# Quarter products for w_v, and the next batch's mixing placed inside the w_k product

## Chip, cores and metric

One core of a Trainium2 chip runs the whole kernel. The metric is the device time of one execution in microseconds (us). A matmul runs on TensorE (PE; its weight loads are PEld), element-wise work on VectorE (DVE), ScalarE (ACT) and GpSimd (POOL); transfers are issued from SyncE's queue (SPq) and ScalarE's (ACTq).

## What is computed

Three layers follow one another on 8 batches of 576 tokens. All matrices are float32.

```
x   = rmsnorm(q @ (k^T v)) * g                      # per head, 8 heads of 64 -> 512 features
xk  = mu_k*x + (1-mu_k)*x_prev                      # x_prev: x one token earlier
xr  = mu_r*x + (1-mu_r)*x_prev
kk  = max(xk @ w_k, 0)                              # w_k: 512 x 1024
x2  = sigmoid(xr @ w_r) * (kk*kk @ w_v)             # w_r: 512 x 512, w_v: 1024 x 512
out = mixture of 4 causal attention experts of x2   # top 2, weights from a gate
```

## The kernel before

A float32 matmul is replaced by three matmuls of the float32r type: each operand x is split into a high part (ScalarE rounds it) and a low part (VectorE subtracts: `split`, L58), and high*high, high*low and low*high are summed in PSUM (`mm3`, L62). The work runs in three stages.

`phase_a` (L174) goes over the batches. `front(b)` (L242) forms k^T v (40 products from five pairs of loads kt, vt), applies it to q in four bursts (`heads`, L268), sums squares with TensorE (`means`, L285), computes the reciprocal root on VectorE in 14 small operations (`rsqrt`, L295) and multiplies it into the tile xT (`scaled`, L316, which spreads the root over partitions by TensorE, L321). `mix_r(b)` makes xr in the tiles xrh, xrl (four rounds of L356 on ScalarE, L357 on VectorE, then a split); `mix_k(b)` makes xk and its operands. `r_group` (L411) is a gate: 12 matmuls, a sigmoid and, per pair of halves, a store to sgd; a batch has eight. `k_pair` (L425) is the w_k product, a Strassen form with seven quarter products instead of eight: weights as seven blocks A11 to S3 and operands b11, b21, t1, t2, b22, t4, t3, of which the t's are differences of quarters of xk, made on GpSimd (L382). A quarter product for one m is 6 matmuls of 288 columns; four m's times seven make 168 in a batch. VectorE adds the quarter results (L457 to L472), GpSimd clips them at zero (L445) and squares them (L446), and they are stored to kkd.

In the loop over batches (L530) batch b's mixing and gates come first; then the w_k product runs, with `front(b+1)` and, from its 20th step on, `mix_r(b+1)` interleaved step by step. `mix_k(b+1)` comes in the next turn. The tiles xT, xk, xrh, xrl and the operands have one buffer each. The weights arrive as 64-bit words and are rebuilt as float32 pairs by `Conv` (L111): one `tick` works on a piece of 128 x 512 with five VectorE operations (L129 to L138), an absolute value on ScalarE, and either three matmuls ("PE") or two GpSimd operations ("POOL", L161 and L162). w_v's eight pieces are converted in the last turn, after the weights' staging pool has been closed (L560, ticks at L539, L555 and L613).

`phase_v` (L573) multiplies kk*kk with w_v directly: for each batch, two halves of the tokens times four m's, each a group of 24 matmuls (8 K tiles times three) of 288 columns; four operand splits of 128 x 1152 (L593, L595) prepare a batch, and VectorE multiplies each group with its gate (L605). x2d is stored by halves. `phase2` (L627) is the attention stage.

Instructions are written in the order of the generators, and `schedule_with_timeline_sim=True` (L989) lets a planner reorder them on each engine by its own estimate of when each is ready; the program order is the priority. On the chip every engine then runs its list in order.

Of the kernel before, what the change touches and what calls it, by code (L numbers as in the profile page):

```python
# [1 line left out]

# [22 lines left out]
def tile_kernel(ctx: ExitStack, tc: tile.TileContext, qT, k, v, g2, mu_k, mu_r, w_r, w_k, w_v, w_qk, w_vg, w_o, out):  # L25
# [21 lines left out]
    kkd = [dram.tile([P, KF, S], F32, name=f"kkd{i}") for i in range(B)]  # L47
    sgd = [dram.tile([P, KD, S], F32, name=f"sgd{i}") for i in range(B)]
# [62 lines left out]
    class Conv:  # L111


        def __init__(self, pool, wts, bufs):
            self.pool, self.wts, self.bufs = pool, wts, bufs
            self.raws, self.cvs, self.ops, self.at = {}, {}, [], 0

        def load(self, i):
            if i < len(self.wts):
                _, _, w, r0, c0, _ = self.wts[i]  # L120
                raw = self.raws[i] = self.pool.tile([P, CW, 2], I32, name="raw", bufs=self.bufs)
                nc.scalar.dma_start(raw.rearrange("p n t -> p (n t)"), w[r0:r0 + P, c0:c0 + CW].bitcast(I32))

        def words(self, i):
# [9 lines left out]
            nc.scalar.activation(wh, t, AF.Copy)  # L134
# [10 lines left out]
        def tick(self, acc_tile=None, idn=None):  # L145
            i = self.at
            self.at += 1
            if 0 < i <= len(self.wts):
# [11 lines left out]
                else:  # L160
                    nc.gpsimd.tensor_sub(x, x, h.bitcast(F32))  # L161
                    nc.gpsimd.tensor_add(l, x, l.bitcast(F32))  # L162
                self.load(i - 1 + self.bufs)
            if i < len(self.wts):
                t = self.cvs[i] = self.pool.tile([P, CW], F32, name="cvt", bufs=self.bufs)
# [8 lines left out]
    def phase_a():  # L174
        with ExitStack() as st1:
# [20 lines left out]
            a21h = stg.tile([P, 2, 512], F32R, name="a21h")  # L196
            a21l = stg.tile([P, 2, 512], F32R, name="a21l")
# [5 lines left out]
            for blk, r0, c0 in ((A11, 0, 0), (A12, 2, 0), (None, 0, 512), (A22, 2, 512)):  # L203
                for i in range(2):
                    h, l = (a21h, a21l) if blk is None else (wkh[:, blk], wkl[:, blk])
# [3 lines left out]
            def sums(i):  # L209
# [3 lines left out]
                a21 = [(a21h[:, i, :], 1), (a21l[:, i, :], 1)]  # L213
# [140 lines left out]
            def mix(b, p, mu, nu, x):  # L354
                xT = xTs[b]
                nc.scalar.activation(x, xT[:, p, 0:S], AF.Copy, scale=nu[:, p:p + 1])  # L356
                nc.vector.scalar_tensor_tensor(x, xT[:, p, 1:S + 1], mu[:, p:p + 1], x, op0=ALU.mult, op1=ALU.add)  # L357

            def mix_r(b):
                for p in range(KD):  # L360
                    x = sb.tile([P, S], F32, name="xm", bufs=2)
                    mix(b, p, mur, nur, x)
                    split(xrh[:, p, :], xrl[:, p, :], x)
# [3 lines left out]

            def mix_k(b):
# [149 lines left out]
            for i in range(8):  # L518
                r_group(0, *divmod(i, 2))
                run(mk)  # L520
                if i < 6:
                    tick()
# [470 lines left out]
```

## Time and profile before

| | us |
|---|---|
| median of 3 runs (lowest, highest) | 1171.03 (1170.14, 1173.21) |
| the profiled execution, its own time | 1171.94 |
| its span | 1170.1 |
| PE busy | 1017.1 (87%) |
| DVE busy | 617.7 (53%) |
| ACT busy | 486.9 (42%) |
| POOL busy | 436.0 (37%) |

The busy shares are means over stages with different limits, so they say little; the stages have to be read one by one. Matmuls overlap in the trace: a 288-column matmul is shown with 0.29 us, while the next one starts some 0.13 us later at full clock. The page's idle columns tell what ended each wait.

### The profile page before, as it was taken

The page shows a single profiled execution, that of the slowest core. Times are in us where ns is not written, and L with a number is a line of the kernel's source. Part 1 is how long each engine was busy: PE and PEld are TensorE (multiplying, and loading weights), DVE is VectorE, ACT ScalarE, POOL GpSimd, SP SyncE. Part 2 cuts the span into 40 slices and gives each one's busy share as a digit, 9 for nine tenths or more (in the row PEclk, how much of TensorE's full clock was granted, in tenths as well). Part 3 has the DMA queues.
Part 4 walks back from the last instruction along what each step waited for, and adds up shares of the span by engine and source line. Part 5 has one row for each costly group of instructions (what it writes and reads, how often), then busy time and mean ns, then how long its engine had stood idle before and what let it go on. Part 6 is the DMA issues. An engine that isn't in the chain of part 4 may idle for free.

```text
span 1170.1 us, 20536 instructions
## 1 busy us (share of the span) xinstructions
PE 1017.1 (87%) x7968; PEld 909.9 (78%) x7968; DVE 617.7 (53%) x1508; ACT 486.9 (42%) x1123; POOL 436.0 (37%) x456
## 2 busy tenths in 40 slices
PE   5459796978879796959699999989999999999998
PEld 3248685858777685858599999988888988889887
DVE  5682645455463627288845333315656565565553
ACT  4454443534353534444313112104554463554544
POOL 0021645463636455468910000014453262352521
PEclk8679898988979798989789999999999999999999
DMA  9304242433324151225856655312020120210102
GB/s 317 120 1 144 100 143 102 140 104 113 111 83 161 63 169 53 84 77 181 329 166 233 200 185 163 97 64 60 23 82 24 60 80 4 81 52 32 64 1 81
DMA packets 59312, 127.17 MB, mean 109 GB/s; under 512 B 5712, under 2 KB 23632, under 8 KB 56144
## 3 DMA queue, kind: packets, MB, share of 16 engines
q1 hardware_dynamic: 47888, 105.94, 26.5%
q10 hardware_dynamic: 11328, 19.93, 5.4%
q8 instruction: 63, 1.03, 0.4%
q14 instruction: 33, 0.27, 0.1%
HBM read 78.66 MB, written 47.19 MB: 108 GB/s over the span
## 4 chain that ended last, share of the span: by engine, by line
PE 59%; DVE 16%; POOL 11%; DMA 8%; ACT 5%; issue 3%; ACTq 0%; SPq 0%; POOLq 0%; DVEq 0%
PE acc L64 12%; PE acc L66 11%; PE acc L65 11%; PE acc L434 11%; POOL tk L382 4%; DMA x2in<-x2d 3%; PE pt L812 3%; PE acc L839 2%; POOL so L445 2%; DVE xk L357 2%; DVE xT L324 2%; POOL x2l L649 2%; PE s L763 2%; PE po L275 2%; DMA vt<-in_v 2%
## 5 line engine op out<-in xcount | busy, mean ns | idle before, releaser
L445 POOL TENSOR_SCALAR so<-so 128x576 f32<-128x576 f32 x64 | 108.7, 1702 | 140.4 <-DVE so L463 126.7
L65 PE MATMUL acc<-kkl,wvh 128*128 128x288 f32 x512 | 153.9, 301 | 5.5 <-DVE kkl L595 5.5
L66 PE MATMUL acc<-kkh,wvl 128*128 128x288 f32 x512 | 153.5, 301 | 3.8 <-POOL wvl L162 3.8
L64 PE MATMUL acc<-kkh,wvh 128*128 128x288 f32 x512 | 153.0, 299 | 3.8 <-ACT kkh L593 3.8
L792 POOL TENSOR_SCALAR pr<-pr,rc,wg 128x512 f32<-128x512 f32 (+3 forms) x128 | 76.3, 608 | 98.5 <-DVE wg L722 61.7
L775 ACT ACTIVATE pr<-pr,nm 128x256 f32<-128x256 f32 (+4 forms) x144 | 83.2, 579 | 66.3 <-DVE nm L729 63.1
L65 PEld LDWEIGHTS acc<-kkl,wvh 128*128 128x128 f32 x512 | 99.0, 193 | 6.1 <-DVE kkl L595 6.1
L66 PEld LDWEIGHTS acc<-kkh,wvl 128*128 128x128 f32 x512 | 98.7, 193 | 4.3 <-POOL wvl L162 4.3
L64 PEld LDWEIGHTS acc<-kkh,wvh 128*128 128x128 f32 x512 | 98.8, 193 | 4.2 <-ACT kkh L593 4.0
L321 PE MATMUL po<-rb,selb 32*128 32x144 f32 x128 | 22.2, 435 | 77.2 <-DVE rb L314 44.0
L593 ACT ACTIVATE kkh<-kin 128x1152 fp32r<-128x1152 f32 x32 | 37.1, 1166 | 123.8 <-PE acc L66 112.2
L65 PE MATMUL acc<-xrl,wrh 128*128 128x288 f32 x256 | 78.3, 318 | 8.9 <-DVE xrl L60 8.8
L64 PE MATMUL acc<-xrh,wrh 128*128 128x288 f32 x256 | 69.8, 347 | 14.0 <-ACT sg L419 11.7
L321 PEld LDWEIGHTS po<-rb,selb 32*128 32x128 f32 x128 | 16.7, 303 | 83.4 <-issue 83.4
L64 PE MATMUL acc<-x2h,wqh 128*128 128x256 f32 (+1 forms) x256 | 79.8, 312 | 1.4 <-DVE vs L692 1.0
L65 PE MATMUL acc<-x2l,wqh 128*128 128x256 f32 (+1 forms) x256 | 76.9, 300 | 4.3 <-POOL x2l L649 4.3
L605 DVE TENSOR_TENSOR sgv<-acc,sgv 128x288 f32<-128x288 f32 x64 | 28.9, 455 | 94.4 <-PE acc L66 94.4
L66 PE MATMUL acc<-xrh,wrl 128*128 128x288 f32 x256 | 77.3, 314 | 0.0
L66 PE MATMUL acc<-x2h,wql 128*128 128x256 f32 (+1 forms) x256 | 76.6, 299 | 0.0
L446 POOL TENSOR_TENSOR so<-so 128x576 f32<-128x576 f32 x64 | 75.2, 1184 | 2.5
L729 DVE CUSTOM_DVE_ANT_0 pr<-s,mask 128x256 f32<-128x256 f32 (+4 forms) x144 | 66.9, 482 | 16.4 <-PE pt L812 12.1
L382 POOL TENSOR_TENSOR tk<-xk 128x576 f32<-128x576 f32 x16 | 26.6, 1661 | 107.2 <-DVE xk L357 104.4
(235 smaller groups left out, 3000.5 us busy)
## 6 DMA issues: line engine op xcount, KB each, us to landing
kkd<-so SPq DMA_DIRECT2D x64, 288.0 KB, 2.1
kin<-kkd SPq DMA_DIRECT2D x16, 1152.0 KB, 6.2
qt<-in_qT SPq DMA_DIRECT2D x32, 288.0 KB, 2.9
sgd<-sg SPq DMA_DIRECT2D x32, 288.0 KB, 2.2
sgv<-sgd SPq DMA_DIRECT2D x8, 1152.0 KB, 5.3
x2d<-sgv SPq DMA_DIRECT2D x16, 576.0 KB, 3.6
out<-ob SPq DMA_DIRECT2D x28, 288.0 KB, 2.1
kt<-in_k SPq DMA_DIRECT2D x24, 256.0 KB, 4.3
```

The costliest lines, as they stand in the source:

```text
L64: nc.tensor.matmul(ps, wh(i), xh(i), start=(i == 0), stop=False)
L65: nc.tensor.matmul(ps, wh(i), xl(i), start=False, stop=False)
L66: nc.tensor.matmul(ps, wl(i), xh(i), start=False, stop=(i == n - 1))
L321: nc.tensor.matmul(po[:, c, i * QS:(i + 1) * QS], selb[g, 2 * a + i, :], rb[g], start=True, stop=True)
L382: eng.tensor_sub(t, x, y)
L434: nc.tensor.matmul(bank[:, :HS], w[:, blk, i, ms_], x[:, i, :], start=(start and i == 0 and n == 0), stop=(stop and i == 1 and n == 2), sk ...
L445: nc.gpsimd.tensor_scalar(x, x, 0.0, None, op0=ALU.max)
L446: nc.gpsimd.tensor_mul(x, x, x)
L593: nc.scalar.activation(hi, x, AF.Copy)
L729: nc.vector.tensor_tensor_reduce(out=pr[:R, k0:k0 + kn], in0=s[:R, :kn], in1=mk, scale=1.0, scalar=lo, op0=ALU.add, op1=ALU.min, accum_out ...
L775: nc.scalar.activation(pr[:, :L], pr[:, :L], AF.Exp, bias=nm, scale=-1.0, accum_out=sms[b, p, j][:, e2:e2 + 1])
L792: nc.gpsimd.tensor_scalar(pr[:, :L], pr[:, :L], rc[:, r:r + 1], wg, op0=ALU.mult, op1=ALU.mult)
```

## The change

In `phase_v`, w_v is cut into four blocks of 512 x 256, from which seven are made (a11, a12, s1, s2, s4, a22, s3; the sums on GpSimd, each block split into high and low), and each batch is computed by seven quarter products of K = 512: 2 m's times 12 matmuls each, 168 a batch in place of 192. The operands t1, t2 (VectorE) and t4, t3 (GpSimd) are differences of quarters of kk*kk, each operand is split (seven splits of 128 x 1152 in place of four), five buffers hold high and five low parts, and the output is joined by VectorE and gated on GpSimd. x2d is stored once a batch.

In `phase_a`, `front(b+1)` starts in the gates of batch b, and `mix_r(b+1)` and the whole of `mix_k(b+1)`, differences included, follow inside the w_k product of batch b; only the seven operand splits stay beside the gates. The clipping moves from GpSimd to ScalarE. w_v is converted in 16 half pieces in the w_k products of batches 1 to 5 and parked in DRAM (wvd). For batch 0, the mixing and the gates go by halves of the tokens, front(1) starts before the weights' sums, and the w_k product does the two quarter products that need no sums first, for all m.

```diff
 class Conv:
-            nc.scalar.activation(wh, t, AF.Copy)
+            if way == "PE":
+                nc.scalar.activation(wh, t, AF.Copy)
+            else:
+                wl = self.lows[i] = self.pool.tile([P, self.cw], F32, name="cvl", bufs=1)
...
-                    nc.gpsimd.tensor_sub(x, x, h.bitcast(F32))
-                    nc.gpsimd.tensor_add(l, x, l.bitcast(F32))
+                    nc.gpsimd.tensor_add(x, x, self.lows.pop(i - 1))
+                    nc.sync.dma_start(h, x)
...
 def mix_k(b):
+                kin[b, "xk"] = sb.tile([P, KD, S], F32, name="xk")
+                def diff(name, x, y):
+                    t = kin[b, name] = sb.tile([P, 2, HS], F32, name="tk", bufs=4)
+                    nc.gpsimd.tensor_sub(t, x, y)
+                    return t
+                for p in range(KD):
+                    mix(b, p, muk, nuk, kin[b, "xk"][:, p, :])
+                    if p == 1:
+                        t1 = diff("t1", quarter(b, 0, 1), quarter(b, 0, 0))
+                    yield
+                t2 = diff("t2", quarter(b, 1, 1), t1)
+                yield
+                diff("t4", t2, quarter(b, 1, 0))
+                yield
+                diff("t3", quarter(b, 1, 1), quarter(b, 0, 1))
+                yield
+            def operands(b):
+                for name in ("b11", "b21", "t1", "t2", "b22", "t4", "t3"):
+                    x = quarter(b, int(name[1]) - 1, int(name[2]) - 1) if name[0] == "b" else kin[b, name]
+                    h, l = [w1.tile([P, 2, HS], F32R, name=f"{name}{u}") for u in "hl"]
+                    split(h, l, x)
+                    kops[b, name] = (h, l)
+                    yield
...
 def k_pair(b, m):
-                so = lt.tile([P, 2, 2, HS], F32, name="so", bufs=3)
+                    so = lt.tile([P, 2, HS], F32, name="so", bufs=4)
-                    nc.gpsimd.tensor_scalar(x, x, 0.0, None, op0=ALU.max)
+                    nc.scalar.activation(x, x, AF.Relu)
                     nc.gpsimd.tensor_mul(x, x, x)
...
             for b in range(B):
+                f = f1 if b == 0 else front(b + 1) if nxt else None
                 if b > 0:
+                    mk = operands(b)
                     for i in range(8):
                         r_group(b, *divmod(i, 2))
+                        run(mk, f)
+                    for _ in mk:
+                        pass
+                prods = [k_pair(b, m) for m in range(KD)]
+                if b == 0:
+                    steps = [x for p in prods for x in [p[0]] * 2] + [x for p in prods for x in [p[1]] * 5]
+                else:
+                    steps = [x for p in prods for x in [p[0]] * 2 + [p[1]] * 5]
                 mr = None
+                for n, x in enumerate(steps):
+                    run(x)
+                    if nxt:
+                        if n < 12:
+                            run(f)
+                        elif n == 12:
+                            for _ in f:
+                                pass
+                            mr = chain(mix_r(b + 1), mix_k(b + 1))
+                        run(mr)
+                    if 0 < b < 6 and n in (15, 18, 21, 24) and cw.at <= len(cw.wts):
+                        cw.tick()
...
 def phase_v():
+            def block(name, x, pool):
+                h, l = [pool.tile([P, KH, HM], F32R, name=f"w{u}_{name}") for u in "hl"]
+                split(h, l, x)
+                blk[name] = (h, l)
...
+                def operand(name, x):
+                    h, l = [sb.tile([P, KH, HS], F32R, name=f"kk{u}", bufs=5) for u in "hl"]
+                    split(h, l, x)
+                    ops[b, name] = (h, l)
+                def diff(x, y, eng):
+                    t = sb.tile([P, KH, HS], F32, name="tv", bufs=3)
+                    eng.tensor_sub(t, x, y)
+                    return t
...
+                def prod(q, w, x, m, start, stop):
+                    (wh, wl), (xh, xl) = blk[w], ops[b, x]
+                    ms_ = slice(m * P, (m + 1) * P)
+                    for i in range(KH):
+                        for n, (a, c) in enumerate(((wh, xh), (wh, xl), (wl, xh))):
+                            nc.tensor.matmul(q[:, :HS], a[:, i, ms_], c[:, i, :], start=(start and i == 0 and n == 0),
+                                             stop=(stop and i == KH - 1 and n == 2), skip_group_check=True)
+                def gated(i, m, h, op, x, y):
+                    c = sb.tile([P, HS], F32, name="ct", bufs=3)
+                    op(c, x, y)
+                    g = sg[:, 2 * i + m, h * HS:(h + 1) * HS]
+                    nc.gpsimd.tensor_mul(g, c, g)
...
+                nc.sync.dma_start(x2d[b], sg)
```

## Rows read from the trace of the kernel before

**Rows 1.** Head of the profile's page, whole span.

```profile
span 1170.1 us, 20536 instructions
```

**Rows 2.** Windows: start:end, length, busy per engine (x count), clock, DMA share, GB/s.

```profile
0.00:105.00 105.00, 63.28 (x380) 42.56 (x380) 64.02 (x130) 48.20 (x83) 9.48 (x21) 0.79 0.40 136
130.50:191.95 61.45, 51.93 (x446) 46.04 (x444) 31.82 (x59) 26.94 (x53) 32.70 (x22) 0.92 0.34 114
191.95:203.52 11.57, 2.54 (x17) 1.91 (x16) 9.37 (x23) 3.77 (x7) 5.50 (x4) 0.73 0.23 87
203.52:220.85 17.33, 15.17 (x98) 14.70 (x97) 12.90 (x18) 11.01 (x21) 9.30 (x5) 0.89 0.09 35
500.10:556.95 56.85, 42.60 (x281) 40.26 (x280) 49.41 (x80) 27.11 (x55) 40.00 (x23) 0.88 0.36 129
556.95:781.70 224.75, 211.27 (x1538) 209.74 (x1537) 92.73 (x130) 46.69 (x52) 31.25 (x28) 0.95 0.54 184
```

**Rows 3.** Waits of TensorE, 105 to 534 us: total, times, longest.

```profile
PE po L321 <- DVE xT L324: 30.9, 21, 2.2
PE po L321 <- DVE rb L314: 30.2, 7, 4.6
```

**Rows 4.** Timeline of TensorE, 196 to 204 us; last bracket: idle before, releaser.

```profile
196.62 0.44 PE L321 MATMUL po<-rb,selb 32*128 32x144 f32 x4 [4.61 <-DVE rb L314]
```

**Rows 5.** Timeline of VectorE, 760 to 770 us.

```profile
762.16 0.46 DVE L605 TENSOR_TENSOR sgv<-acc,sgv 128x288 f32<-128x288 f32 x1 [2.72 <-PE acc L66]
765.34 0.46 DVE L605 TENSOR_TENSOR sgv<-acc,sgv 128x288 f32<-128x288 f32 x1 [2.71 <-PE acc L66]
```

**Rows 6.** Timeline of TensorE, 92.9 to 106 us.

```profile
93.19 0.40 PE L218 MATMUL acc<-a21h,idp 128*128 128x512 f32 x1
...
105.07 1.15 PE L253 MATMUL acc<-vt,kt 128*64 128x64 f32 x31
```

**Rows 7.** Timeline of TensorE, 161 to 170 us: start, duration, what.

```profile
161.23 1.15 PE L253 MATMUL acc<-vt,kt 128*64 128x64 f32 x32
...
169.62 0.71 PE L275 MATMUL po<-qt,kv 64*64 64x288 f32 x8
```

**Rows 8.** Timeline of VectorE, 203 to 207 us.

```profile
204.12 0.75 DVE L60 TENSOR_TENSOR xrl<-xm,xrh 128x576 fp32r<-128x576 f32 x1
204.79 0.93 DVE L324 SCALAR_TENSOR_TENSOR xT<-xT,g_sb,po 128x288 f32<-128x288 f32 x2
205.65 1.13 DVE L60 TENSOR_TENSOR xrl<-xm,xrh 128x576 fp32r<-128x576 f32 x1
```

**Rows 9.** Timeline of GpSimd, 203 to 216 us.

```profile
204.28 1.87 POOL L382 TENSOR_TENSOR tk<-xk 128x576 f32<-128x576 f32 x1 [5.45 <-DVE xk L357]
210.45 4.55 POOL L382 TENSOR_TENSOR tk<-xk,tk 128x576 f32<-128x576 f32 x1 [4.29 <-DVE xk L357]
...
215.08 1.41 POOL L382 TENSOR_TENSOR tk<-xk 128x576 f32<-128x576 f32 x1
```

**Rows 10.** Timeline of VectorE, 57 to 63 us: first and last of 14.

```profile
57.95 0.31 DVE L299 TENSOR_SCALAR ms<-acc 64x144 f32<-64x144 f32 x1 [6.43 <-PE acc L292]
...
62.15 0.37 DVE L314 SCALAR_TENSOR_TENSOR rb<-rb,lom,y 64x144 fp32r<-64x144 f32 x1
```

**Rows 11.** Timeline of VectorE, 5 to 9 us.

```profile
5.44 0.43 DVE L129 TENSOR_SCALAR cvt<-cvt 128x512 f32<-128x512 f32 x1 [2.92 <-ACT cvt L166]
...
6.36 0.69 DVE L133 SCALAR_TENSOR_TENSOR cvt<-raw,cvt 128x512 int32<-128x512 int32 x1
```

**Rows 12.** Groups over the whole span: line, operation, shapes, count, busy, mean ns.

```profile
L446 POOL TENSOR_TENSOR so<-so 128x576 f32<-128x576 f32 x64 | 75.2, 1184 | 2.5
...
L595 DVE TENSOR_TENSOR kkl<-kin,kkh 128x1152 fp32r<-128x1152 f32 x32 | 46.6, 1462 | 29.4 <-ACT kkh L593 29.4
...
L593 ACT ACTIVATE kkh<-kin 128x1152 fp32r<-128x1152 f32 x32 | 37.1, 1166 | 123.8 <-PE acc L66 112.2 <-issue 8.9 <-DVE wvl L138 1.8
```

**Rows 13.** Timeline of TensorE, 555 to 575 us.

```profile
560.71 0.61 PE L64 MATMUL acc<-kkh,wvh 128*128 128x288 f32 x1 [3.76 <-ACT kkh L593]
```

More of the change, by code (lines that the diff above doesn't have):

```diff
@@ L1 @@
 from contextlib import ExitStack
+from itertools import chain
 import concourse.bass as bass
@@ L47, in tile_kernel @@
     kkd = [dram.tile([P, KF, S], F32, name=f"kkd{i}") for i in range(B)]
+    wvd = dram.tile([P, KF, DM], F32, name="wvd")
     sgd = [dram.tile([P, KD, S], F32, name=f"sgd{i}") for i in range(B)]
@@ L476, in phase_a @@
+                return first(), rest()
             for c in "w0 w1 w2 k0 k1 k2 q0 k3 q1 q2".split():
@@ L524, in phase_a @@
+            mk = operands(0)
+            for _ in range(7):
+                run(mk, f1)
+            tick()
             for i in range(2):
                 for _ in sums(i):
-                    pass
+                    run(f1)
             stg_.close()
-            late.append(st1.enter_context(tc.tile_pool(name="late", bufs=1, reuse_waits="tile")))
+            lt = st1.enter_context(tc.tile_pool(name="late", bufs=1, reuse_waits="tile"))
+            late.append(lt)
+            HC = 256
@@ L578, in phase_v, with part @@
-            kin, ops, sgt = {}, {}, {}
+            KH = KF // 2
+            HM = DM // 2
+            val = vv.tile([P, KF, DM], F32, name="val")
+            for i in range(2):
+                nc.sync.dma_start(val[:, KH * i:KH * i + KH, :], wvd[:, KH * i:KH * i + KH, :])
+            blk = {}
+            def part(i, j):
+                return val[:, KH * j:KH * j + KH, HM * i:HM * i + HM]
+            def block(name, x, pool):
+                h, l = [pool.tile([P, KH, HM], F32R, name=f"w{u}_{name}") for u in "hl"]
+                split(h, l, x)
+                blk[name] = (h, l)
@@ new lines, in phase_v @@
+            block("a11", part(0, 0), vw)
+            block("a12", part(0, 1), vw)
+            s1, s2 = [sb.tile([P, KH, HM], F32, name=f"sum{u}") for u in "ab"]
+            nc.gpsimd.tensor_add(s1, part(1, 0), part(1, 1))
+            block("s1", s1, sb)
+            nc.gpsimd.tensor_sub(s2, s1, part(0, 0))
+            block("s2", s2, sb)
+            nc.gpsimd.tensor_sub(s1, part(0, 1), s2)
+            block("s4", s1, sb)
+            block("a22", part(1, 1), sb)
+            nc.gpsimd.tensor_sub(s2, part(0, 0), part(1, 0))
@@ L611, in phase_v @@
                 pass
[L612 to L613 removed]
+            vs.close()
             for b in range(B):
```

325 lines of the change are left out of this document (160 added, 165 removed).

## The prediction

> **What bounds the kernel now.** I read the head of the page for the total [rows 1] and then cut the span into stages [rows 2], because the busy shares mix stages with different limits. One batch of the first stage lasts 61.45 us, from the end of one w_k product to the end of the next. It has three parts: 11.57 us in which PE is busy for 2.54, then 17.33 us of gates, then the rest, 32.55 us, in which PE works on the w_k product and the next batch's front. The waits of PE over seven such batches name the first part: 30.2 us for the root (rb) and 30.9 for the scaled tile xT [rows 3]; one of them is shown at 196.62, 4.61 us idle [rows 4]. So the chain root, scaling, mixing stands bare between two products. The idle stretch also costs clock: granted 0.73 there and 0.89 in the gates behind it, against full clock in a steady product [rows 2].
>
> What PE needs without waits follows from the w_v stage: groups of 24 matmuls end 3.18 us apart [rows 5], so a matmul costs 0.1323 us. A batch's 96 gates are 12.7 us (measured 17.33), the 168 matmuls of the w_k product 22.2, and the four scaling bursts, at the shortest of them, 4 x 0.44 = 1.8 [rows 4]. The PE floor of a batch is 32.55 + 12.7 + 1.8 = 47.0 us.
>
> The other stages: start-up to the first w_k product, 105 us with PE busy 63 [rows 2]; from 500.10 to 556.95, the last batch, with w_v's conversion on top; from 556.95 to 781.70 w_v's product, 224.75 us, PE busy 211; then the attention stage, 1170.1 - 781.7 = 388.4 [rows 1, 2].
>
> **The change part by part, in five pieces of the span.**
>
> *Start-up to the end of product 0.* The first half of the gates (48 x 0.1323 = 6.4 us) goes into time in which PE waits, so the weights' sums start near 93.2 - 6.4 = 86.8. They take until 105.07, 11.9 us [rows 6], mostly latency. The changed order has work for PE there: front(1)'s k^T v (2.5 bursts of 1.15) and q (4 of 0.71), 5.7 us [rows 7], and the eight quarter products that need no sums, 48 x 0.1323 = 6.4; together 12.1. Product 0 and front(1) are 32.55 + 1.8 = 34.3 us of PE, 11.9 of it done, so product 0 ends at 86.8 + 11.9 + 22.4 = 121. Mixing by halves adds instructions but no elements. If no more than half of this cover holds it is 127; if the shorter mixing chain also comes earlier, 113.
>
> *Batches 1 to 5, with pieces of w_v.* The chain goes under the product, and what is late next is the SBUF side of VectorE and GpSimd. The rows show that they exclude each other there: a GpSimd difference of 576 columns takes 1.41 us alone, but 4.55 beside an unbroken run of VectorE operations, and the one issued at 204.28 ends at 206.15, while a VectorE split that takes 0.75 alone takes 1.13 and ends only at 206.78 [rows 8, 9]. Beside L324, which reads PSUM, the GpSimd operation went on [rows 8, 9]. Work in one product stage, then:
> VectorE on SBUF: root 62.15 + 0.37 - 57.95 = 4.6 [rows 10]; eight mixings and four splits, 12 x 0.75 = 9.0 [rows 8]; four w_v ticks: a full piece is three operations of 0.43 and two of 0.69 = 2.67 [rows 11], a half piece, estimated between half of it and the whole, 1.6, so 6.4. Sum 20.0.
> VectorE reading PSUM: 16 joins and 8 scalings at 0.46 [rows 5], 11.0.
> GpSimd: eight squares at 1.18 [rows 12], 9.5; four differences at 1.41, 5.6; four adds of 256 columns, half of 1.18, 2.2. Sum 17.3. (The clipping leaves it.)
> If only SBUF work excludes: 20.0 + 17.3 = 37.3 us. If nothing overlaps: 48.3. PE has some 26 there. I take 37.3, because rows 8 and 9 show the overlap with PSUM reads. To it come the gates, 12.7, and the front's k^T v and q, 5.7, now PE's work beside the gates: 18.4, with 7 x 0.75 of splits on VectorE, so the last mixings (4 x 0.75) and the last difference (1.4) can spill into them: 37.3 + 18.4 - 4.4 = 51.3, taken as 52 for gaps. Bounds: 47 (PE floor) and 48.3 + 18.4 = 66.7.
> The Trainium skill, page "GPSIMD Engine Reference", section "Key points", says that GpSimd shares its SBUF interfaces with VectorE and contends with operations that have two SBUF inputs or run in a two-port mode. By that rule PSUM-reading operations stay free and the stage sums to 37.3; without it the sum would be 48.3. The trace agrees as far as rows 8 and 9 reach.
>
> *Batch 6, no pieces.* 37.3 - 6.4 - 2.2 + 18.4 - 4.4 = 42.7, under the PE floor: 47.
>
> *Last batch.* Gates 12.7 and product 22.2, no mixing and no conversion: 35, taken as 36 against 56.85 now [rows 2]. The w_v blocks (load, four GpSimd sums, seven splits) lie beside it.
>
> *w_v product.* A lead-in remains: the operand's split waits for tiles of the w_k product; now 3.76 us idle [rows 13], and PE then starts at the lower of its two clocks: 5 in all. A batch needs 168 x 0.1323 = 22.2 us of PE. VectorE: seven splits and two differences of 1152 columns at 1.46 [rows 12], 13.1; eight joins at 0.46, 3.7. GpSimd: two differences of twice 1.41, 5.6, and eight gatings of 288 columns, half of 1.18, 4.7; 10.3. SBUF work exclusive: 23.4, just over PE; nothing overlapping: 27.1; full cover: 22.2. I take 23.5: 5 + 8 x 23.5 = 193 (bounds 183 and 222). ScalarE has 7 x 1.17 [rows 12] and eight short copies, well under it.
>
> *Costed at nothing.* Clipping on ScalarE: eight copies of 576 columns, half of 1.17 [rows 12], 4.7 us on an engine busy 26.94 of 61.45 [rows 2]; uncovered, 33 over seven batches. The added stores and loads (wvd 2 MB each way, sgd in eight pieces): DMA share 0.34 [rows 2]. They stand in SyncE's queue with the kkd stores, which wait for GpSimd's squares; behind them the kt, vt and qt loads, for which k^T v and q wait. The earlier front gives these a whole gate stage of lead. x2d in one store: only the last one could matter, and phase2 begins with batch 0.
>
> **The sum.** 121 + 5 x 52 + 47 + 36 + 193 + 388.4 = 1045.4 us of span, against 1170.1. Per piece: 191.95 to 173 up to the end of product 1 (-19), 308.15 to 255 for the next five (-53), 56.85 to 36 (-21), 224.75 to 193 (-32). The profiled execution's own time is 1171.94, 1.8 over its span, and the median 1171.03, 0.9 below it: 1046.
>
> **The rivals.**
> *PE bound everywhere.* The planner spreads VectorE's work well, and pieces cost their half. 113 + 6 x 46.5 + 35 + 183 + 388 = 998. For it: VectorE and GpSimd are busy 31.8 and 32.7 of 61.45 [rows 2], some of it mutual waiting. Against: the SBUF sum of a product stage, 37.3, is well over PE's 26.
> *The mixing does not get under the product.* The planner's order, or GpSimd held off by VectorE's runs (4.55 for 1.41), leaves the chain bare, and w_v is bound by the engines too: batches 61.5, batch 6 50, start-up 127, last batch 38, w_v 206, attention 388: 1117. For it: the product stage would be VectorE's tightest. Against: the clipping leaves GpSimd, and the differences have a whole gate stage before they are needed.
> *Slower.* Seven operands go through five buffers in the w_v product. If each split starts only when the product before it frees its buffer and the matmuls wait for both halves, each of the 56 operands adds 1.17 + 1.46 = 2.63 us [rows 12]: w_v 5 + 178 + 147 = 330, total 1183. It decides from 2.4 us an operand. For it: the first product of w_v waits just so [rows 13]. Against: four operands in the same five buffers cost no wait in the steady state, groups ending 3.18 apart [rows 5], and a split is needed only after four more products.
>
> **How the numbers follow.** The SBUF-bound forecast 0.55 (its own range 1015 to 1080: batches 47 to 57, w_v 22.2 to 25); PE bound 0.19; mixing bare 0.21; slower 0.04; no change 0.01. The range 1000 to 1100 leaves out about 0.08 below and 0.12 above. Faster than 0.3% (about what a measurement here can tell from no change): 0.95; within it 0.01; slower 0.04.
>
> **What the new profile would show.** Right: no PE wait for rb or xT longer than a microsecond after the first batch; batches of about 52 us, the last without pieces near 47; VectorE nearly unbroken in the products of batches 1 to 5, with GpSimd squares and differences of 2 us and more; w_v batches of 23 to 24 us. Wrong: PE unbroken at 46 to 47 throughout (PE bound); gates still waiting for xrl or rb, or ScalarE held by a late t operand with the sigmoids queued behind it (mixing bare); waits of 2 us and more before every w_v product (slower).

## The result and the profile after

The changed kernel takes 1104.8 us (median of four executions, 1102.33 to 1107.45) against 1170.59 for the kernel before, run beside it: a ratio of 0.944 [0.941, 0.947]. That is faster, as forecast, but by 66 us where 125 were forecast, and 4.8 us above the range.

The head of the page, and the row of TensorE's granted clock over the span in 40 slices:

```profile
span 1102.7 us, 20713 instructions
...
PE 992.2 (90%) x7776; PEld 882.6 (80%) x7776; DVE 749.0 (68%) x1603; ACT 575.8 (52%) x1290; POOL 471.2 (43%) x476
...
PEclk8889689799989998997998999999999999999999
```

The profiled execution took 1104.46 us, 1.8 over its span, so the forecast's sum of spans can be laid beside it. The windows of the changed kernel, cut at the first matmul and the end of product 0 and then at the end of each w_k product (columns as in [rows 2]); the last three are the w_v stage:

```profile
95.30:145.50 50.20, 36.94 (x231) 33.92 (x229) 42.60 (x90) 25.05 (x50) 19.96 (x17) 0.76 0.28 91
145.50:192.10 46.60, 43.52 (x385) 38.12 (x384) 30.97 (x81) 21.94 (x52) 17.95 (x18) 1.00 0.69 220
192.10:253.80 61.70, 54.03 (x434) 46.34 (x433) 37.16 (x64) 35.05 (x66) 17.27 (x14) 0.89 0.38 123
253.80:303.70 49.90, 48.47 (x430) 41.92 (x428) 32.62 (x58) 30.33 (x61) 18.35 (x13) 1.00 0.44 143
303.70:359.00 55.30, 51.48 (x453) 45.43 (x452) 37.84 (x60) 32.34 (x63) 18.41 (x14) 0.91 0.38 124
359.00:406.40 47.40, 46.08 (x399) 40.44 (x398) 32.04 (x56) 28.72 (x58) 15.76 (x12) 1.00 0.47 156
406.40:460.70 54.30, 50.48 (x430) 44.73 (x429) 37.03 (x60) 32.70 (x64) 17.96 (x14) 0.91 0.31 105
460.70:504.80 44.10, 37.51 (x262) 36.22 (x260) 21.75 (x35) 22.76 (x45) 19.43 (x12) 0.96 0.24 89
504.80:529.40 24.60, 5.88 (x28) 5.30 (x28) 19.33 (x12) 13.46 (x15) 19.14 (x10) 0.72 0.77 298
529.40:585.00 55.60, 49.65 (x356) 48.94 (x356) 55.60 (x53) 26.04 (x41) 35.53 (x20) 0.96 0.46 159
585.00:715.30 130.30, 130.22 (x959) 130.23 (x960) 118.36 (x98) 57.85 (x81) 109.49 (x59) 0.98 0.49 181
```

By the pieces of the forecast: product 0 ends at 145.5 (forecast 121, +24.5); the next five batches take 260.9 us (260); batch 6 takes 54.3 (47, +7.3), the last batch 44.1 (36, +8.1), the w_v stage 210.5 (193, +17.5), the rest 387.4 (388.4, -1.0). Together +57 of span. The five batches look right in sum, but not one by one: 46.6, 61.7, 49.9, 55.3, 47.4, and the short ones have the full clock. A part of the spread is only where the cuts fall, since PE's share of the front moves across them: the five windows hold 385, 434, 430, 453 and 399 matmuls.

What PE now waits for between 105 and 505 us (total, times, longest), against [rows 3], which were taken from 105 to 534:

```profile
PE acc L66 <- ACT xrh L61: 9.5, 6, 2.3
PE po L324 <- DVE xT L327: 6.7, 5, 2.8
PE acc L67 <- DVE xrl L62: 5.5, 5, 1.5
...
PE acc L66 <- ACT sg L410: 3.3, 1, 3.3
```

The 61 us for root and scaled tile are down to 6.7, all of it for the scaled tile. But the end of the same chain, the mixed operand xrh and xrl, now stands before the gates, once or more in each batch from 2 to 7 (in batch 1, whose mixing ended at 127.6, 18 us before the end of product 0, there is no such wait). The timeline of TensorE at the gates of batch 4 shows how small these waits are:

```profile
315.09 1.81 PE L66 MATMUL acc<-xrh,wrh 128*128 128x288 f32 x6 [2.35 <-ACT xrh L61]
...
319.54 0.61 PE L67 MATMUL acc<-xrl,wrh 128*128 128x288 f32 x1 [1.47 <-DVE xrl L62]
```

They cost more than they last. Here are windows of 5 us at the gates of batch 6, where the same waits stand:

```profile
411.40:416.40 5.00, 4.12 (x32) 3.28 (x32) 5.00 (x6) 2.44 (x5) 3.20 (x2) 1.00 0.39 123
416.40:421.40 5.00, 2.98 (x14) 1.77 (x14) 5.00 (x5) 3.96 (x7) 3.60 (x4) 0.58 0.08 29
421.40:426.40 5.00, 4.08 (x17) 4.08 (x18) 3.54 (x5) 1.27 (x3) 0.25 (x1) 0.50 0.00 0
426.40:431.40 5.00, 5.00 (x38) 4.40 (x38) 0.00 (x0) 3.38 (x9) 0.00 (x0) 0.90 0.48 164
```

PE stands 2 of 5 us, the granted clock falls to its lower level (0.50), and 14 and 17 matmuls are done in the time of 38 at 0.90. VectorE is unbroken meanwhile. Its timeline at the gates of batch 2, and GpSimd's beside it:

```profile
202.27 1.53 DVE L360 SCALAR_TENSOR_TENSOR xk<-xT,muk,xk 128x576 f32<-128x576 f32 x2
203.73 0.74 DVE L62 TENSOR_TENSOR t1l<-tk,t1h 128x576 fp32r<-128x576 f32 x1
204.40 3.85 DVE L360 SCALAR_TENSOR_TENSOR xm<-xT,mur,xm 128x576 f32<-128x576 f32 x2
208.16 1.97 DVE L62 TENSOR_TENSOR b21l<-xk,b21h 128x576 fp32r<-128x576 f32 x1
```

```profile
203.94 1.79 POOL L382 TENSOR_TENSOR tk<-xk,tk 128x576 f32<-128x576 f32 x1 [3.55 <-DVE xk L360]
205.81 1.81 POOL L382 TENSOR_TENSOR tk<-tk,xk 128x576 f32<-128x576 f32 x1
207.59 1.93 POOL L382 TENSOR_TENSOR tk<-xk 128x576 f32<-128x576 f32 x1
```

Two mixings take 3.85 us where two took 1.53 just before, and a split 1.97 where one alone takes 0.74: the two engines go turn about, as [rows 8, 9] let expect, and they do it in the tail of the chain for which the gates wait.

And the pieces of w_v are not where the diff writes them. These are windows of line 131 alone, the first VectorE operation of a piece (length, busy, count, clock, DMA share, GB/s):

```profile
95.30:145.50 50.20, 3.91 (x7) 0.76 0.28 91
145.50:192.10 46.60, 3.57 (x9) 1.00 0.69 220
192.10:253.80 61.70, 0.00 (x0) 0.89 0.38 123
```

All 16 pieces lie in the stages of products 0 and 1: the planner, which reorders each engine's work by its own costs, pulled them forward from batches 1 to 5.

### The profile page after: what moved, and what is told of

It reads as the page before. It is cut to its first block, busy times and chain, and to the rows that moved or that the text cites. A ratio compares the mean times of both kernels' runs of the same rounds, so it can differ in the third digit from the quotient of the medians.

```text
span 1102.7 us, 20713 instructions
## 1 busy us (share of the span) xinstructions
PE 992.2 (90%) x7776; PEld 882.6 (80%) x7776; DVE 749.0 (68%) x1603; ACT 575.8 (52%) x1290; POOL 471.2 (43%) x476
## 3 DMA queue, kind: packets, MB, share of 16 engines
q1 hardware_dynamic: 47792, 110.13, 28.9%
## 4 chain that ended last, share of the span: by engine, by line
PE 39%; POOL 5%; issue 4%; DVE 4%; ACT 3%; DMA 3%; ACTq 0%; POOLq 0%; DVEq 0%
PE acc L666 13%; PE acc L66 6%; PE acc L67 5%; PE acc L68 5%; PE pt L916 3%; PE acc L943 3%; DMA x2in<-x2d 3%; PE s L867 2%; POOL x2l L753 2%; ACT pr L879 2%; DVE kkl L62 1%; POOL pr L896 1%; POOL so L435 1%; ACT x2h L752 1%; PE s L852 1%
## 5 line engine op out<-in xcount | busy, mean ns | idle before, releaser
L678 POOL TENSOR_TENSOR sgv<-ct,sgv 128x288 f32<-128x288 f32 x64 | 92.0, 1464 | 33.9 <-DVE ct L676 33.8
L666 PE MATMUL acc<-kkh,wh_s 128*128 128x288 f32 x256 | 77.0, 302 | 5.7 <-DVE ct L676 5.7
L666 PE MATMUL acc<-kkl,wh_s 128*128 128x288 f32 x256 | 76.7, 300 | 0.0
L666 PE MATMUL acc<-kkh,wl_s 128*128 128x288 f32 x256 | 76.4, 299 | 0.0
L66 PEld LDWEIGHTS acc<-xrh,wrh 128*128 128x128 f32 x256 | 51.3, 211 | 26.8 <-ACT xrh L61 11.3
L666 PE MATMUL acc<-kkh,wh_a 128*128 128x288 f32 x192 | 57.7, 302 | 11.4 <-ACT kkh L61 11.4
L666 PE MATMUL acc<-kkl,wh_a 128*128 128x288 f32 x192 | 58.5, 304 | 7.6 <-DVE kkl L62 7.6
L67 PEld LDWEIGHTS acc<-xrl,wrh 128*128 128x128 f32 x256 | 52.7, 207 | 15.0 <-DVE xrl L62 11.4
L916 PE MATMUL pt<-ident,pr 128*128 128x128 f32 x400 | 62.6, 276 | 0.6
L434 ACT ACTIVATE so<-so 128x576 f32<-128x576 f32 x64 | 43.2, 680 | 32.0 <-DVE so L460 25.2
```

The source lines that it names most:

```text
L66: nc.tensor.matmul(ps, wh(i), xh(i), start=(i == 0), stop=False)
L67: nc.tensor.matmul(ps, wh(i), xl(i), start=False, stop=False)
L434: nc.scalar.activation(x, x, AF.Relu)
L666: nc.tensor.matmul(q[:, :HS], a[:, i, ms_], c[:, i, :], start=(start and i == 0 and n == 0), stop=(stop and i == KH - 1 and n == 2), skip_ ...
L678: nc.gpsimd.tensor_mul(g, c, g)
L916: nc.tensor.transpose(pt[:, (i - i0) * P:(i - i0 + 1) * P], pr[:, k1 - P:k1], ident)
```

## The experiments

Medians are of four executions, of five for all_held_plain and kk_early; ratios are to the kernel before, run beside them. "Batch 3: 48" is the time from the end of product 2 to the end of product 3 in that run's profile.

**1. Two buffers for xT.** First theory: the one xT tile closes a loop, since q of the next front is written over it when mixing ends (PE began with q at 264.2, 311.0, 366.2, 413.8; the last mixings ended at 264.3, 315.1, 366.2, 417.8; in the second and the fourth of these q began 4 us before the last mixing ended, which speaks against the theory).

```diff
-                xT = sb.tile([P, NP, S + 1], F32, name="xT")
+                xT = sb.tile([P, NP, S + 1], F32, name="xT", bufs=2)
```

Room came from kt and vt with three buffers; the second run has that alone, and the third takes the room from sg (three) and the w_v pieces (one buffer).

> The changed kernel with two buffers for xT; to make room, kt and vt have three buffers in place of four, and are loaded three chunks ahead. Theory: from batch 2 on the batches of the first stage are bound by a loop through the one xT tile (mixing of a batch ends, the next front's q is written over it, root, scaling, mixing: 264.3 to 315.1 to 366.2 to 417.8 to 467.9, 51 us each), not by the SBUF side of VectorE and GpSimd. Then with two buffers q is written under the gates' first half or before, mixing ends inside the product, and the batches 2 to 6 fall from a mean of 53.7 us to 47 to 49: total 1070 to 1085. Rival (the forecast's step, VectorE and GpSimd excluding each other at SBUF): the work is the same, batches stay at 52 to 54 and the total within 8 us of the changed kernel's 1104.8.

> The control for the run with two xT buffers: only kt and vt with three buffers, loaded three chunks ahead. Theory: within 4 us of the changed kernel's 1104.8 in either direction. Rival: the prefetch of kt and vt is what counts (PE waits 10 us for vt in the changed kernel), and fewer buffers cost 8 us or more.

> The buffers of early_front (two xT, sg three, one piece buffer) with the order of the change. Theory (buffers alone change nothing, as with xt_two): batches 2 to 6 at a mean of 51 to 55, total 1095 to 1120. Rival (the room, the one piece buffer above all, gave the gain of early_front): total 1085 or less.

Measured: xt_two 1129.9 us, ratio 0.963 [0.960, 0.967]; kv_three 1117.8, 0.954 [0.952, 0.956]; two_xt_room 1111.6, 0.948 [0.947, 0.950]. All three are slower than the changed kernel. In all three batches 5 and 6 take 52.1 or 52.2 us, and batches 3 to 6 of the changed kernel average 51.7. A second buffer alone changes nothing in them: the first theory has no support here. kv_three missed its expectation of no change by 13 us; that fewer kt and vt buffers cost 8 us or more was its rival. (xt_two is 12 us over kv_three, and its w_v stage takes 223.9 us for 208.8.)

**2. The pieces left out, and the pieces held.**

For no_pieces the ticks go and wvd is filled by eight copies of parts of w_qk, so that the later stages work on other numbers:

```diff
-                        for i in range(2):
-                            cw.load(i)
-                    if 0 < b < 6 and n in (15, 18, 21, 24) and cw.at <= len(cw.wts):
-                        cw.tick()
+                        for i in range(KF):
+                            nc.sync.dma_start(wvd[:, i, :], w_qk[(i % KD) * P:(i % KD + 1) * P, :])
```

For held_pieces each load is preceded by a write from the newest kept tile of the running product, and the first loads move into batch 1:

```diff
+                if self.after is not None:
+                    nc.scalar.activation(raw[:, 0, 0:1].bitcast(F32), self.after[:, 0:1], AF.Copy)
```

> The changed kernel without the conversion of w_v: no loads of the pieces, no VectorE and GpSimd operations on them, no stores; instead eight copies of w_qk from DRAM to DRAM stand in wvd, so that the later stages do the same work on other numbers. Theory: the planner pulled all 16 pieces into the products of batches 0 and 1, so their price is paid there alone: the end of product 1 comes at 165 to 178 in place of 192.1, batch 2 falls from 61.7 to 51 to 56, batches 3 to 7 stay within 1.5 us, total 1072 to 1088. Rival (the forecast's step): the pieces are part of a sum that fills products 1 to 5, and five batches fall by 5 us each, product 0 by little.

> The changed kernel with the pieces of w_v held in their batches: before each load one element of its buffer is written from the newest kept tile of the running product, so that no piece can be loaded, and so converted, ahead of batches 1 to 5. Theory: product 0 and the gates behind it get free of them (end of product 1 at 168 to 180 in place of 192.1), and the pieces fall into idle time of VectorE in later batches, which are bound by the loop through xT: batches 2 to 5 grow by 0 to 3 us each, total 1082 to 1100. Rival (SBUF side binds): each batch with pieces grows by 6 us and more, and the total stays at 1104 or above.

Measured: no_pieces 1120.9, ratio 0.957 [0.954, 0.959]: slower than with the work. held_pieces 1111.9, 0.949 [0.946, 0.953]. Both expectations missed. Without pieces product 0 begins at 107.3 instead of 95.3, and batches 2 to 6 take 56.6, 56.3, 44.0, 58.0, 58.2. The run does not tell what the pieces cost: its own eight copies are issued between 14.8 and 28.4 us, in a start-up whose DMA share is 0.90 from 20 to 40 us (0.74 in the changed kernel), and they may have delayed it. Held, product 1 ends 7 us earlier (185.1), but batches 2 to 5 take 61.7, 58.3, 53.5, 50.7, together 10 us more. So in this order holding the pieces gains nothing, and a planner that orders anew with every edit moves a part by 10 us. What follows is read from batches, not from totals.

**3. The front one stage earlier.** Second theory: the chain q, means, root, scaling, mixing is longer than the product in which it is written. In the changed kernel the last q of the front written in batch 4 ends at 332.1, 2 us into the product, means at 336.2; scaling runs from 346.3 to 360.7, 1.7 past the product's end, mixing until 366.2.

```diff
+                f2 = front(b + 2) if b + 2 < B else None
...
-                        if n < 12:
+                        n0 = 2 if b else 12
+                        if n < n0:
...
+                        if 18 <= n < 26:
+                            run(f2)
```

> Two xT buffers (room from sg with three buffers and the w_v pieces with one), and the order written one stage earlier: k^T v and q of batch b+2 in the last third of the product of batch b, means, root and scaling in the gates of b+1, mixing from the third step of the product of b+1. The two xT buffers alone changed nothing in the batches (52.2 us each, as with one), since the front's place in the written order stayed. Theory: a batch is PE's floor of 47 us plus a wait at the head of the gates, because the chain from q through means, root, scaling and mixing is longer than the product it lies in (q still runs 7 us into the product, xT is ready 6 us behind its end); with a gate stage of slack the wait goes and batches 2 to 6 fall from 53.7 to 47 to 49: total 1070 to 1085. Rival (the forecast's step, work of VectorE and GpSimd at SBUF fills the stage): batches stay at 51 to 54, total 1095 to 1110.

Measured: 1078.5, ratio 0.920 [0.917, 0.922], 26 us under the changed kernel. Batches 3 to 7 take 48.2, 49.5, 49.1, 41.3, 35.4 (batch 6 has no front in it any more, so its 41.3 is not to be compared). The early part pays for it: product 1 ends at 203.2 for 192.1, product 2 at 259.0 for 253.8. The windows of batches 4 and 5:

```profile
307.20:356.80 49.60, 48.00 (x427) 41.87 (x427) 34.70 (x60) 30.76 (x62) 18.36 (x13) 1.00 0.45 145
356.80:405.80 49.00, 47.60 (x426) 41.50 (x425) 33.81 (x59) 30.07 (x61) 18.35 (x12) 1.00 0.32 107
```

PE is busy all but 1.5 us, at the full clock. Against the changed kernel this run alters buffers and order together. Against two_xt_room, which has the same buffers, it alters the written order alone: 33 us less in all, and batches 3 to 5 fall from 56.4, 53.7, 52.1 to 48.2, 49.5, 49.1. The next run has the order with one xT buffer.

> The order of early_front (front one stage earlier) with the one xT buffer of the change, all else as in early_front. Theory (the loop goes through xT: q of batch b+2 can be written only when batch b+1 is mixed, and that now lies in the next product): batches 2 to 6 are back at 51 to 55 us, total 1095 to 1115. Rival (the place in the written order alone did it): batches at 47 to 50, total 1082 or less.

Measured: 1090.8, ratio 0.931 [0.929, 0.932]. Batches 3 to 7: 48.2, 49.5, 49.0, 41.3, 35.4, the same as with two buffers; the 12 us of difference lie in the start-up (product 1 ends at 208.5 for 203.2), the w_v stage and the rest. My theory of the loop through xT is wrong; the rival holds for the batches (its total, 1082 or less, was missed): the place in the written order did it.

**4. The differences on VectorE.**

```diff
-                    nc.gpsimd.tensor_sub(t, x, y)
+                    nc.vector.tensor_sub(t, x, y)
```

> The changed kernel with the four differences of a batch in mix_k on VectorE in place of GpSimd. In the changed kernel's trace they go turn about with the last mixings: a mixing of 0.80 us takes 1.96 beside a difference of 1.8, and xrl's splits, for which the gates wait, stand behind. Theory (they shut each other out of SBUF, and it is the tail of the chain that pays): VectorE gets 4 x 0.74 us more and loses 4 x 1.16 of waiting, the gates start 1 to 4 us earlier, total 1080 to 1100. Rival (VectorE is the bound by its own work): batches grow by 3 us, total 1115 to 1125.

> The front one stage earlier and, with it, the four differences of mix_k on VectorE. Alone they gave 26 and 15.6 us. Theory (a batch is PE's floor plus the wait for the chain's tail; the front's move alone has brought the steady batches to 49 us with PE busy 48.6 of 50): there is no tail left that the differences could shorten, so they add 0 to 5 us, out of the first batches: total 1073 to 1079. Rival (the mutual shutting out of VectorE and GpSimd is a bound of its own in every batch): the two gains add, total 1060 to 1066.

Measured: diffs_vector 1089.2, ratio 0.929 [0.927, 0.930]; early_diffs 1066.4, 0.910 [0.908, 0.911]. Alone they give 15.6 us, with the early front 12 of these again: more than my theory allowed, less than a full sum. Batches 3 to 5 are 47.8, 47.1, 47.1 with PE busy throughout, 0.4 to 2.4 less than in early_front; batch 2 gains 5.0 (50.8 for 55.8) and the early part 2.1. Both readings hold a part.

**5. The stage that the forecast summed.** Mixing under the product, differences and squares on GpSimd, pieces of w_v on VectorE in batches 1 to 5:

> The front one stage earlier and the w_v pieces held in batches 1 to 5, with mix_k's differences on GpSimd as in the change: this is the stage as the blind forecast summed it, mixing under the product, differences and squares on GpSimd, pieces on VectorE. The forecast's step (SBUF work of VectorE and GpSimd excludes itself and fills the stage): batches 2 to 4 take 52 us, total 1070 or more. Theory (the stage is PE's, the exclusion costs only where a chain's tail is bare): batches 2 to 4 take 48 to 50.5 us, total 1055 to 1068.

Measured: 1083.7, ratio 0.924 [0.921, 0.926]. The windows of batches 2 to 5; the last has all but no pieces:

```profile
200.30:253.80 53.50, 49.72 (x426) 43.02 (x425) 42.56 (x80) 32.33 (x69) 21.33 (x17) 0.94 0.53 163
253.80:307.80 54.00, 50.23 (x426) 43.39 (x426) 42.22 (x79) 32.09 (x69) 21.33 (x17) 0.94 0.50 162
307.80:360.40 52.60, 48.85 (x426) 42.54 (x425) 40.47 (x75) 31.99 (x68) 21.30 (x17) 0.97 0.52 165
360.40:408.70 48.30, 47.43 (x425) 41.11 (x423) 37.34 (x69) 29.20 (x61) 19.01 (x14) 1.00 0.38 121
```

My theory missed, and the forecast's step is right for this stage: 52 us with pieces, 47 without, against 53.4 and 48.3. VectorE is all but unbroken in the product, as the forecast's sign has it; here is product 3 but for its first 3 us:

```profile
268.80:307.80 39.00, 35.23 (x295) 30.45 (x295) 37.65 (x67) 24.51 (x50) 18.71 (x14) 0.91 0.43 147
```

What PE loses lies at the product's end. There it waits for xrl (9.8 us in seven waits between 200 and 409 us), for gates that the planner put into the product, and its clock falls:

```profile
PE acc L67 <- DVE xrl L62: 9.8, 7, 2.3
```

```profile
298.80:303.80 5.00, 3.18 (x13) 2.47 (x14) 5.00 (x5) 2.20 (x5) 2.77 (x2) 0.65 0.23 88
```

The forecast's sum also says what the differences on VectorE should do: 4 x 0.75 more there, 5.6 less on GpSimd, so 49.4; the runs all_held below measure 48.1.

**6. Product 0 in the plain order.**

```diff
-                if b == 0:
-                    steps = [x for p in prods for x in [p[0]] * 2] + [x for p in prods for x in [p[1]] * 5]
-                else:
-                    steps = [x for p in prods for x in [p[0]] * 2 + [p[1]] * 5]
+                steps = [x for p in prods for x in [p[0]] * 2 + [p[1]] * 5]
```

> The changed kernel with product 0 written in the order of the other products (each m's two products without sums followed by its five with them), in place of all first parts ahead of all second parts. In the changed kernel product 0 takes 50.2 us from its first matmul, four of six PSUM banks are held by the first parts, and PE waits 2.8, 4.1 and 4.0 us for joins (so) on VectorE, at a granted clock of 0.57 to 0.67. Theory (the four held banks make every join urgent): product 0 takes 32 to 42 us, its end comes 4 to 12 us earlier, total 1093 to 1101. Rival (VectorE is full, 20.0 of 20 us from 115 to 135, with the next batch's mixing whatever the order of the products; joins stand behind it in its queue): product 0's end stays within 3 us, total 1101 to 1108.

Measured: 1101.4, ratio 0.939 [0.938, 0.941]. Product 0 takes 32.0 us for 50.2 and ends at 128.6, but batches 1 and 2 take 56.1 and 63.0: by the end of product 2 the gain is 6.2 us. The order made product 0 slow. That the chain of the next batch takes the time back is a reading of the stages and no run isolates it; in all, the kernel hardly differs from the changed one (0.939 against 0.944 [0.941, 0.947]).

**7. The w_v stage.**

In blocks_vector one of the four sums looks so, the others and t4 and t3 of batch 0 alike; the last line is the edit of weights_late, ahead of each load of wst, where W["late"] is an element of batch 6's kk.

```diff
-            nc.gpsimd.tensor_add(s1, part(1, 0), part(1, 1))
+            nc.vector.tensor_add(s1, part(1, 0), part(1, 1))
...
+            nc.scalar.activation(st[:, 0:1], W["late"], AF.Copy)
```

> The changed kernel with the four sums of w_v's blocks on VectorE in place of GpSimd, and so the two GpSimd differences of the first w_v operand set. In the changed kernel the first 24.7 us of the w_v stage hold 5.9 us of PE work: sums of 2.3 to 3.4 us on GpSimd, and splits of 1.2 us that take 2.4 to 3.8 beside them. Theory: without the mutual waiting the blocks are ready 8 to 12 us earlier, w_v stage 198 to 203 in place of 210.5, total 1092 to 1098. Rival (the lead-in is the loads of kkd and the serial chain of sums): the lead-in stays within 3 us, total 1101 to 1109.

> The changed kernel with the last stage's weights held: one element of each wst buffer is first written from batch 6's kk tile, so their loads, scalings and splits come in the second half of the w_v stage and not in its first 55 us. Theory: of the 10 us that the stretch from 529.4 to 585.0 takes over its PE work, the 6 of waits for VectorE (ct, kkl) go: total 1096 to 1101. Rival: the later batches, in which VectorE is busy 118 of 130 us, take the same work and give the gain back, total 1102 to 1108.

Measured: blocks_vector 1100.7, ratio 0.940 [0.937, 0.943], w_v stage 204.2 us; weights_late 1103.5, 0.940 [0.938, 0.943], stage 206.3. Both totals missed their theories (1092 to 1098, 1096 to 1101), and their intervals overlap that of the changed kernel; the stage alone falls by 6 and 4 us. In blocks_vector PE still begins so:

```profile
517.49 0.85 PE L666 MATMUL acc<-kkh,wh_a 128*128 128x288 f32 x2 [12.80 <-ACT kkh L61]
520.26 0.85 PE L666 MATMUL acc<-kkh,wh_a 128*128 128x288 f32 x2 [1.93 <-ACT kkh L61]
```

**8. Together.** all_float has the early front, the differences, sums and first w_v differences on VectorE and the late weights; all_held holds the pieces too; all_held_plain adds the plain order of product 0; kk_early loads the first half of batch 0's kk ahead of the last product:

```diff
+            kin = {(0, 0): vv.tile([P, KH, S], F32, name="kin0")}
+            nc.sync.dma_start(kin[0, 0], kkd[0][:, 0:KH, :])
...
-            block("a12", part(0, 1), vw)
+            block("a12", part(0, 1), sb)
```

> The front one stage earlier, the differences of mix_k, the block sums and the first two w_v differences on VectorE, and the last stage's weights held until batch 6's kk tile: everything that gained alone, the w_v pieces left to the planner. Theory: early_front with its differences, 1073 to 1079, less 6 for the block sums and 2 to 4 for the weights: total 1062 to 1071. Rival (the gains of the w_v stage come out of the same wait for the loads of kkd): 1070 to 1076.

> As all_float, and the w_v pieces held in the products of batches 1 to 5. Theory: VectorE has room beside a PE-bound product (35 of 50 us busy in early_front), so the pieces cost nothing there and product 0 and the gates behind it lose 15 us of VectorE work: 4 to 10 us under all_float. Rival (each held piece adds its SBUF time to the product, 6.4 us in four batches): 5 us and more over all_float.

> As all_held, with product 0 written in the order of the other products. Alone this ended product 0 17 us earlier (128.6 for 145.5), and product 1 and batch 2 gave 13 of them back, because the next batch's chain did not come earlier. Theory: with the front a stage ahead and no pieces there, less is given back, total 1036 to 1043. Rival (product 1 waits for the chain of batch 1 whatever product 0 does): within 2 us of all_held's 1045.5.

> As all_held_plain, and the first half of kk of batch 0 is loaded for the w_v stage together with val, ahead of the last w_k product (it takes the room of block a12, which moves to the other pool). With the block sums on VectorE the w_v stage still begins with a wait of 12.8 us for kk's first split, and its load stands in SyncE's queue behind the last stores of kkd. Theory: this load is the rest of the lead-in; the stage falls from 199.8 us to 189 to 194, total 1030 to 1036. Rival (the blocks' splits and the operands' low parts on VectorE are as late): 197 us or more, total 1037 to 1042.

Measured: all_float 1060.6, ratio 0.906 [0.904, 0.908]; all_held 1045.5, 0.892 [0.891, 0.894]; all_held_plain 1039.7, 0.886 [0.884, 0.887]; kk_early 1043.0, 0.890 [0.889, 0.892]. Batches of all_held with pieces:

```profile
187.70:235.80 48.10, 47.23 (x422) 41.19 (x423) 39.21 (x82) 30.85 (x68) 14.59 (x13) 1.00 0.56 181
235.80:283.90 48.10, 47.61 (x426) 41.41 (x425) 39.76 (x82) 31.69 (x69) 13.94 (x13) 1.00 0.58 181
```

Held, the pieces gain 15 us over all_float, more than the 4 to 10 expected: product 1 ends at 187.7 for 198.3, and the batches with them take one microsecond more than those without (47.1). kk_early missed: the w_v stage takes 201.4 us for 199.8. Its expectation took the 12.8 us from blocks_vector; in all_held_plain, from which it differs, the first wait was already 5.39 us and the next 2.25. In kk_early the first is hardly shorter and the second is longer:

```profile
457.07 0.85 PE L678 MATMUL acc<-kkh,wh_a 128*128 128x288 f32 x2 [4.97 <-ACT kkh L61]
464.83 0.85 PE L678 MATMUL acc<-kkh,wh_a 128*128 128x288 f32 x2 [6.92 <-ACT kkh L61]
```

The fastest version is all_held_plain, 65 us under the changed kernel.

## Why the prediction was wrong

**Direction right, mechanism in part.** The waits for root and scaled tile between two products went, and the time fell; the end of the same chain, mixing and splits, stayed before the gates.

**The step that failed first: "the chain goes under the product, and what is late next is the SBUF side".** I summed a stage as if the planner would run the chain inside it, and never laid the chain's own steps end to end. The rows for it were there: root 4.6 us alone [rows 10], then scaling, mixing and splits, after means that wait for the last q, which the diff leaves in the gates. In the changed kernel this chain ends behind the product from batch 2 on, by 7 to 16 us up to the last mixing. The wait went from rb and xT to xrh and xrl, as my rival "mixing bare" said in kind; its time, 1117, was nearer than the forecast's, but by luck (batches of 61.5 where the mean was 52.2, a start-up of 127 where it was 145.5). Shown by early_front against two_xt_room: with the chain written a stage earlier and nothing else changed, batches 3 to 5 fall from 52 to 56 us to 48 to 49.5 (early_one_xt has the same batches with one buffer). By size this step stands openly in 15 of the 57 us, in batches 6 and 7; the other 42 are start-up and w_v stage, two terms that I sized wrongly.

**Batches 1 to 5: a right sum for a wrong reason.** 260.9 us against 260, but no batch after 1 held a piece of w_v, and VectorE, forecast nearly unbroken, was busy 15.5, 19.4 and 15.5 us of the 28.6, 28.9 and 28.5 of products 3 to 5. The sum as such stands: where the pieces really are in the products (early_held), 53.4 against 52, with VectorE busy 37.7 of 39 us. The error was to take the written place of the pieces for the place of their work.

**Batch 6 (+7.3) and the last batch (+8.1).** In batch 6 it is the same bare tail, with no pieces to hide the error. In the last batch xrh and xrl cost 1.7 us of waits, and the longest wait is another, 3.3 us for a gate's output tile:

```profile
477.42 0.40 PE L66 MATMUL acc<-xrh,wrh 128*128 128x288 f32 x1 [3.33 <-ACT sg L410]
```

```profile
476.38 0.68 ACT L61 ACTIVATE t2h<-tk 128x576 fp32r<-128x576 f32 x1 [5.34 <-POOL tk L382]
```

```profile
467.36 7.64 POOL L435 TENSOR_TENSOR so<-so 128x576 f32<-128x576 f32 x2 [6.23 <-issue]
474.96 1.39 POOL L382 TENSOR_TENSOR tk<-xk,tk 128x576 f32<-128x576 f32 x1
```

The sigmoids stand on ScalarE behind a split that waits for a difference, and the difference stands on GpSimd behind two squares that take 7.64 us, for 2.4 alone [rows 12], while VectorE runs on. This is the sign that the prediction gave for "mixing bare". With the early front the last batch takes 35.4, against 36.

**Start-up (+24.5): mis-sized.** I put the sum-free matmuls under the weights' sums and then 22.4 us of bare product. The first part came nearly so. The sums end at 99.1, forecast 98.7, with 20 of the 48 sum-free matmuls begun; this is the last of them:

```profile
98.76 0.39 PE L221 MATMUL acc<-wkl,idn 128*128 128x512 f32 x1
```

What was left took 46.4 us for 22.4. Windows of 10 us in it, and the longest wait of its timeline:

```profile
115.00:125.00 10.00, 5.25 (x22) 4.85 (x22) 10.00 (x19) 6.62 (x12) 4.93 (x4) 0.57 0.33 112
125.00:135.00 10.00, 6.85 (x30) 6.62 (x30) 10.00 (x13) 6.47 (x12) 7.95 (x6) 0.66 0.09 34
```

```profile
128.02 0.61 PE L424 MATMUL acc<-t4h,wkh 128*128 128x288 f32 x1 [4.09 <-DVE so L460]
```

VectorE is full with the next batch's scaling and mixing and the pulled-forward pieces; the joins that free PSUM stand behind them. plain_order shows the larger cause: writing the first parts of all four m ahead of all second parts costs 18 us of product 0. Without it batches 1 and 2 take most of that time back. Where the chain too is early and the pieces are held, the plain order brings 5 us (end of product 1 at 182.5 in all_held_plain, 187.7 in all_held).

**The w_v stage (+17.5): the lead-in.** The steady part is better than forecast: 960 matmuls in 130.3 us, 22.8 us a batch for 23.5. PE is busy 130.2 us of it, so PE binds there and not the SBUF sum of 23.4 from which I took my figure. But the 384 matmuls before it, 52.1 us at that pace, took 80.2: a lead-in of 28 us where I gave 5. I had priced only the wait for the operand's buffers [rows 13], not the block sums on GpSimd with splits beside them, nor the load of kk, which SyncE issues behind the last stores:

```profile
504.99 3.85 SPq L436 DMA_DIRECT2D kkd<-so  x3
508.89 0.92 SPq L618 DMA_DIRECT2D kin<-kkd  x2
```

The sums, with the first two differences, are worth 6 us of it and the last stage's weights 4 (blocks_vector, weights_late). That the load's place is worth more was only argued, and kk_early, which moves half of it, gained nothing: what binds the rest stays open.

**The other rivals.** PE bound everywhere (998) did not come, though its batches of 46.5 are near the 47.1 of early_diffs. Waits of 2.63 before every w_v product (1183) did not come: the steady part has none.

## What to carry to other kernels

Before a chain is put "under" a long product, add up the chain's own steps from the last operand that it waits for, and compare that with the product; if it is longer, move its beginning one stage earlier, not its end. Where a planner orders the work, what is written in a batch is no evidence that it runs there: hold it with a data dependence, or price it where it is free to go. And a sum over engines that shut each other out is worth making, but it assumes a full stage; look also at where the chain's tail lies, since there the same exclusion is paid twice, in the wait and in the clock.

## What was not expected of the hardware

In batches 4 and 6 two waits of 2.35 and 1.47 us in a gate stage of 26 went with a spell at the lower clock (in batch 6 0.58, then 0.50 over 5 us each), and batch 2, with waits of 2.1 and 1.4, had one too; in batches 3 and 5, where the longest such wait was 0.8, the granted clock stayed at 1.00. Batches of 46.6 to 49.9 us at the full clock alternate with 54.3 to 61.7 at 0.89 to 0.91. That the waits bring the spell is read from these rows; no run changes the one without the other.

Turn about with GpSimd differences, a VectorE mixing takes 1.9 us (two in 3.85) and a difference 1.8; alone they take 0.77 and 1.41 [rows 9]. The Trainium skill, page "SBUF — State Buffer", section "SBUF: two separate sides", says that the port pair these engines share is a lock held for a whole instruction and no split of bandwidth. The rows agree with it, each instruction lasting nearly as long as both alone, though an even split of bandwidth could look the same in them. Nor do the engines always take turns: the two squares of the last batch took 7.64 us beside VectorE's run. Moving the four differences to VectorE shortens a batch with pieces by 5 us (early_held 53.4, all_held 48.1).
